# Seven half products for eight in the second channel product of two token tiles, with the cycles dealt anew

## The chip, the cores and the metric

The kernel runs on one core of a Trainium2 chip. Its time is the device time of one execution in microseconds (us). Before the change it is 352.02 us, the median of three runs (351.7 to 352.77).

## What is computed

For each of 8 batches, 12 heads, 448 positions and head size 64, sigmoid attention is followed by a token mixer and a channel mixer, without normalisation:

```python
scores = scale * np.matmul(q, k.transpose(0, 1, 3, 2)) - np.log(S)
x = np.matmul(1.0 / (1.0 + np.exp(-scores)), v)      # heads side by side: [8, 448, 768]
h = np.maximum(x.transpose(0, 2, 1) @ w_tok1, 0.0) @ w_tok2   # 448 -> 256 -> 448
u = x + h.transpose(0, 2, 1)
out = u + np.maximum(u @ w_ch1, 0.0) @ w_ch2         # 768 -> 1536 -> 768
```

The operands of TensorE are fp16, sums are fp32, and the output is fp32.

## The kernel before

A batch is cut into 3 units `u` of four heads. A **cycle** is one unit of one batch; there are 24. The order of all instructions is written out by hand: the kernel emits them in the order in which each engine is to run them, so an instruction that waits holds up everything behind it on its own engine.

In cycle (b, u), `qk` (L178) makes seven score tiles: four 64x64 matmuls each into one of two PSUM buffers of two banks (tag `qk`), and a sigmoid on ScalarE (L190) that reads the buffer out. `av` (L200) forms attention times values for the unit before in two of four other banks (`m0` to `m3`), and VectorE copies it to `xT` (L219, L223). `xtrans_dma` (L232) transposes it to `xn` by DMA from the queue of SyncE (SP). `tok_tail` and `tok1` (L257, L275) form the first token product of the unit two cycles back from `xn`; ScalarE applies the relu (L300). `ytrans` (L302) closes the cycle with the second token product, which VectorE adds to `xT` to give `ut` (L316).

After the three units, `utrans` (L321) transposes `ut` to `un` by DMA, `token_sums` (L419) forms four differences of it on VectorE, and `sevens` (L935) runs the first channel product, already as seven half products (Strassen's scheme in Winograd's form: 126 matmuls, L488), at the end of cycle u = 2. Its results leave PSUM through ScalarE (L509, L511) and VectorE (L518, L521) as `h2`.

The **second channel product** of a batch (its "lot") runs two batches later, one token tile of 128 rows per cycle. `ch2_pair` (L576) does the two column halves of tile t in cycle u = t: 64 matmuls of 64x64 in which the two halves share the array (`quads`, L356), and 16 of 128x128 (`rest`, L596). `ch2_out` (L558) adds `un` on VectorE (L561) and stores the tile. The last 64 tokens follow in cycle 2 (`ch2_last`, L611). A product of 128x128 stationary by 384 moving columns is called a **unit product** below: four 64x64 matmuls of L364 make one, one matmul of L599 or L538 is one. Tiles 0 and 1 of a lot take 2 x 2 x 12 = 48.

The loop of L1003 holds the steady cycles 9 to 23 (b = 3 to 7, lots 1 to 5), L1058 to L1092 the tail with lots 6 and 7. Lot 0 is done in cycles 5 to 8 (L875, L945), where VectorE also makes the weight sums for `sevens` (`weight_sums`, L398).

The **SP queue** issues, in one order, all `xn`, `un`, `tr_k` and `tr_q` transposes and the stores. In cycle u = 2 the order is `tr_k`, `un`, `xn`, two stores of tile 2, two of the last tokens, `tr_q`. A copy on GpSimd, the **gate** (L860), waits for `tr_q` and then lets the next loads go: v of batch b + 1, k and q of batch b + 2.

Of the kernel before, what the change touches and what calls it, by code (L numbers as in the profile page):

```python
# [21 lines left out]
NJ = 7  # L22
# [8 lines left out]
def kernel(  # L31
# [43 lines left out]
    diffs = pc.tile([128, 4, NU, NS], FP16, name="diffs")  # L75
    xTs = [pc.tile([128, NU, 2, 512], FP16, name=f"xT{n}") for n in range(2)]

    uts = [pc.tile([128, NDB, 512], FP16, name=f"ut{n}") for n in range(2)]
# [121 lines left out]
    def av(b, u, j0=0, j1=NJ):  # L200
        if j0 == 0:
            xa[b, u] = [
                bank([128, 512], FP32, f"xa_{b}_{u}_{g}")
                for g in range(2)
            ]
        ps = xa[b, u]
        for j in range(j0, j1):
            for g in range(2):
                for hi in range(2):
                    nc.tensor.matmul(  # L210
                        out=ps[g][64 * hi : 64 * hi + 64, 0:S],
                        lhsT=raw[b, "v"][64 * g : 64 * g + 64, u, hi, j, :],
                        rhs=att[b, u, j][64 * g : 64 * g + 64, hi, :],
                        start=(j == 0),
                        stop=(j == NJ - 1),
                    )
        if j1 == NJ:
            for g in range(2):
                nc.vector.tensor_copy(  # L219
                    out=xTs[b % 2][:, u, g, 0:S], in_=ps[g][:, 0:S]  # L220
                )
            if NU * b + u >= N_FIRST:
                nc.vector.tensor_copy(  # L223
                    out=xTs[b % 2][:, u, :, S:512], in_=xTs[b % 2][:, u, :, S - 64 : S]
                )


    def xn_tile(b, u):
        xn[b, u] = pa.tile([128, 2, 4, 128], FP16, tag="xn", bufs=3, name=f"xn_{b}_{u}")
        return xn[b, u]  # L230

    def xtrans_dma(b, u):  # L232
        nc.sync.dma_start_transpose(
            out=xn_tile(b, u).rearrange("s g t d -> s (g t) d"),
            in_=xTs[b % 2][:, u, :, :].rearrange("d g s -> d (g s)"),
        )

    def xtrans(b, u):
        ps = bank([128, 4, 2, 128], FP16, f"xb_{b}_{u}")
        for g in range(2):  # L240
            for t in range(4):
                nc.tensor.transpose(
                    out=ps[:, t, g, :],
                    in_=xTs[b % 2][:, u, g, 128 * t : 128 * t + 128],
                    identity=ident[:, :],
                )
# [55 lines left out]
    def ytrans(b, u, banks=()):  # L302
        for g in range(2):
            db = NU * g + u
            if banks:
                at_bank[0] = banks[g]
            ps = bank([128, 512], FP32, f"yt_{b}_{db}")
            for tcb in range(2):
                nc.tensor.matmul(  # L309
                    out=ps[:, 0:S],  # L310
                    lhsT=h1[b, u][:, tcb, g, :],
                    rhs=w2[:, tcb, :, :],
                    start=(tcb == 0),
                    stop=(tcb == 1),
                )
            nc.vector.tensor_tensor(  # L316
                out=uts[b % 2][:, db, 0:S], in0=xTs[b % 2][:, u, g, 0:S], in1=ps[:, 0:S], op=ADD
            )


    def utrans(b):  # L321
        un[b] = pa.tile([128, NDB, 4, 128], FP16, tag="un", bufs=2, name=f"un_{b}")
        nc.sync.dma_start_transpose(
            out=un[b].rearrange("s db t d -> s (db t) d"),
            in_=uts[b % 2].rearrange("d db s -> d (db s)"),
        )
# [7 lines left out]
    def ch1(b, cb, d0=0, d1=NDB):  # L334
# [5 lines left out]
        for d in range(d0, d1):  # L340
# [3 lines left out]
                rhs=uts[b % 2][:, BY_UNIT[d], 0:S],  # L344
# [27 lines left out]
    def ch1_pair(b, cb):  # L372
# [3 lines left out]
        def step(turn, n):  # L376
# [7 lines left out]
                lambda p, part: uts[b % 2][part, BY_UNIT[n], 0:S],  # L384
# [33 lines left out]

    def token_sums(b, u0=0, u1=NU):  # L419

        ut = uts[b % 2]
        k1, k2 = slice(u0, u1), slice(NU + u0, NU + u1)
        n1, n2 = slice(0, NS), slice(NS, S)
        t1, t2, t3, t4 = (diffs[:, n, u0:u1, :] for n in range(4))
# [8 lines left out]
    def ch1_seven(b, banks):  # L433
# [3 lines left out]
        ut = uts[b % 2]  # L437
# [16 lines left out]
            4: diffs[:, 3, :, :],  # L454
            5: diffs[:, 0, :, :],
            6: diffs[:, 1, :, :],
            7: diffs[:, 2, :, :],
# [72 lines left out]
    def ch2(b, t, half, n0=0, n1=NCB):  # L530
# [16 lines left out]
        if b not in un:  # L547
            for n in range(NU):
                nc.tensor.matmul(
                    out=ps[:, 128 * n : 128 * n + 128],  # L550
                    lhsT=uts[b % 2][:, NU * half + n, 128 * t : 128 * t + 128],
# [6 lines left out]
    def ch2_out(b, t, half, ps):  # L558
# [10 lines left out]
        if half == 1:  # L569
            for par in range(2):  # L570
                nc.sync.dma_start(
                    out=orow[b, 2 * t + par],
                    in_=outs[b, t][64 * par : 64 * par + 64, :],
                )

    def ch2_pair(b, t):  # L576


        outs[b, t] = pa.tile([128, D], FP32, tag="outs", bufs=3, name=f"o_{b}_{t}")
        ps = [bank([128, 512], FP32, f"c2_{b}_{t}_{p}") for p in range(2)]  # L580
        n_quads = 8

        def step(turn, n):
# [4 lines left out]
                lambda p, part, m: h2[b][  # L588
                    part, BY_GROUP[n], 128 * t + m : 128 * t + m + 64
                ],  # L590
                lambda p, part: c2[part, BY_GROUP[n], DH * p : DH * p + DH],
                n == 0,
                False,
            )

        def rest():  # L596
            for p in range(2):
                for n in range(n_quads, NCB):
                    nc.tensor.matmul(  # L599
                        out=ps[p][:, 0:DH],  # L600
                        lhsT=h2[b][:, BY_GROUP[n], 128 * t : 128 * t + 128],
                        rhs=c2[:, BY_GROUP[n], DH * p : DH * p + DH],
                        start=False,
                        stop=(n == NCB - 1),
                    )
                ch2_out(b, t, p, ps[p])

        turns = [[lambda t=t, n=n: step(t, n) for n in range(n_quads)] for t in range(2)]
        return turns[0], turns[1], rest

    def ch2_last(b, n0=0, n1=NCB):  # L611
# [20 lines left out]
        for n in range(NU if add_on_pe else 0):  # L632
            for g in range(2):
                nc.tensor.matmul(
                    out=ps[g][:, 128 * n : 128 * n + 128],
                    lhsT=uts[b % 2][:, NU * g + n, 384:448],
# [4 lines left out]
        o = pa.tile([128, DH], FP32, tag="outl", bufs=1, name=f"o_{b}_3")  # L641
# [39 lines left out]
    for n in range(2):  # L681
        nc.vector.memset(xTs[n][:, :, :, S:512], 0.0)
# [191 lines left out]
    by_half = sorted(((t, half) for t in range(3) for half in range(2)), key=lambda g: g[1])  # L874
    for c, cb in ((N_FIRST, 3), (N_FIRST + 1, 8)):  # L875
# [15 lines left out]
        for f in turn0:  # L891
            f()
        qk(b, u, 2)
# [26 lines left out]
        else:  # L920
            for w, f in pieces_ch2(0, by_half[:2]):
                f()
                if copies:
                    copies.pop(0)()
            while copies:
# [9 lines left out]
    def sevens(b, banks=(2, 3, 0, 1, 0)):  # L935
        step = ch1_seven(b, banks)
        for at, (n, gs) in enumerate(SEVENS):
            step(n, gs)
            if copies and at in (1, 3):
                copies.pop(0)()  # L940

    pending, copies = [], []
    early = weight_sums()
    lane = [0]
    for c in range(2 * NU, ONE_RUN):  # L945
# [10 lines left out]
        def work(share):  # L956
            goal = 3 * sum(shares[: c - first]) + share * shares[c - first]
            done = 0
            while pending and spent + done < total * goal / 90:
# [5 lines left out]
                done += w  # L965
                if copies:
                    copies.pop(0)()
                elif early:
                    early.pop(0)()
# [32 lines left out]

    for c in range(ONE_RUN, N_CYCLES):  # L1003
        b, u = divmod(c, NU)
        before, ahead = divmod(c - 1, NU), divmod(c - 2, NU)

        X, Y = 2, 0
        at_bank[0] = X  # L1010
        turn0, turn1, rest = ch2_pair(b - 2, u)
        part = len(turn1) * 2 // 3
        qk(b, u, 0)
        qk(b, u, 1)
        for f in turn0:
            f()
        qk(b, u, 2)
        if copies:
            copies.pop(0)()
            copies.pop(0)()  # L1020
        if u == 2:
            utrans(b - 1)
        at_bank[0] = Y
        av(*before, 0, 4)
        qk(b, u, 3)
        av(*before, 4, NJ)
        xtrans_dma(*before)
        if u == 2:
            token_sums(b - 1)
        qk(b, u, 4)  # L1030
        for f in turn1[:part]:
            f()
        qk(b, u, 5)
        for f in turn1[part:]:
            f()
        at_bank[0] = Y
        tok_tail(*ahead)
        qk(b, u, 6)
        tok1(*ahead, with_scores=True)
        rest()  # L1040
        if u == 1 and copies:
            copies.pop(0)()
            copies.pop(0)()
        if u == 0 and LATER < b + 1 < B or u == 1 and b + 1 == LATER:
            copies = through_dma(b + 1, 0)
        if u == 2:
            at_bank[0] = Y + 1
            for w, f in pieces_last(b - 2):
                f()
            sevens(b - 1)  # L1050
# [4 lines left out]
    assert not copies  # L1055


    c, lot = N_CYCLES, B - 2  # L1058
    groups = [(t, half) for t in range(3) for half in range(2)]
    work = [f for w, f in [*pieces_ch2(lot, groups), *pieces_last(lot)]]  # L1060
    before, ahead = divmod(c - 1, NU), divmod(c - 2, NU)
    at_bank[0] = X
    for f in work[:4]:
        f()
    av(*before)
    xtrans_dma(*before)
    for f in work[4:12]:
        f()
    tok1(*ahead)
    for f in work[12:20]:  # L1070
        f()
    tok1(*before)
    for f in work[20:24]:
        f()
    ytrans(*ahead)
    token_sums(B - 1, 0, 2)
    ytrans(*before)
    utrans(B - 1)
    for f in work[24:]:
        f()  # L1080
    token_sums(B - 1, 2, NU)
    at = at_bank[0]
    m = [(at + n) % 4 for n in range(4)]
    sevens(B - 1, (m[2], m[3], m[0], m[1], m[0]))
    at_bank[0] = m[1]
    for n in range(0, NCB, 3):
        ch2(B - 1, 0, 0, n, n + 3)
    for t, half in groups[1:]:
        for n in range(0, NCB, 3):
            ch2(B - 1, t, half, n, n + 3)  # L1090
# [32 lines left out]
```

## Time and profile before

| | |
|---|---|
| time, median of 3 | 352.02 us |
| profiled execution: time / span | 350.74 us / 349.0 us |
| TensorE (PE) busy | 340.3 us, 98% |
| VectorE (DVE) busy | 201.4 us, 58% |
| ScalarE (ACT) busy | 211.1 us, 60% |
| granted TensorE clock | 1.0 |
| DMA, mean over the span | 52.17 MB, 150 GB/s |

The span runs from the first to the last recorded instruction; the 1.7 us by which the time exceeds it lie around it. Engine shares are averages over an opening that waits for loads (to about 60 us), the steady cycles (102 to 298 us) and a tail. The view of the chain follows the work that ended last back to its releasers: start, length, what.

### The profile page before, as it was taken

Reading aid. Unit: us, or ns where it says so; the run is one execution under the profiler, and the core shown is the slowest. Engines: PE = TensorE matmul, PEld = TensorE weight load, DVE = VectorE, ACT = ScalarE, POOL = GpSimd, SP = SyncE. Lnnn points to the kernel's source line nnn. Section 1 sums busy time; section 2 is a strip of 40 time slices with the busy share of each in tenths; the row PEclk is TensorE's granted clock in tenths of the full one; section 3 lists DMA queues with packets and bytes.
Section 4 is the critical chain, followed back from the end, with each engine's and each line's share of the span. In section 5 each row is a group of like instructions: output and inputs, shape, how many; then the busy total and the mean of one; then the engine's idle time right before and its main releaser. Section 6 shows DMA issues by size and latency. Waiting matters only on the chain.

```text
span 349.0 us, 10254 instructions
## 1 busy us (share of the span) xinstructions
PE 340.3 (98%) x4477; PEld 239.4 (69%) x4477; DVE 201.4 (58%) x401; ACT 211.1 (60%) x271; POOL 57.3 (16%) x98
## 2 busy tenths in 40 slices
PE   7999999999999999999999999999999999999995
PEld 4655566555886679656886679656886679657963
DVE  3376467477765566458575566557574465618621
ACT  4996845587658853988348854888448854111400
POOL 8993430130040000400040000400010000000000
PEclk9999999999999999999999999999999999999999
DMA  8999999999999697998979797998985591064214
GB/s 126 165 165 192 207 204 200 169 203 246 180 183 215 93 191 148 146 185 154 196 131 188 141 190 154 147 185 148 208 124 77 88 167 24 2 121 104 55 47 113
DMA packets 104380, 52.17 MB, mean 150 GB/s; under 512 B 76432, under 2 KB 101264, under 8 KB 104336
## 3 DMA queue, kind: packets, MB, share of 16 engines
q1 hardware_dynamic: 78944, 29.70, 48.8%
q0 software_dynamic: 25168, 21.50, 40.3%
q8 instruction: 35, 0.57, 0.6%
q10 hardware_dynamic: 224, 0.33, 0.3%
q14 instruction: 9, 0.07, 0.1%
HBM read 43.45 MB, written 11.01 MB: 156 GB/s over the span
## 4 chain that ended last, share of the span: by engine, by line
PE 81%; DMA 10%; POOL 4%; ACT 2%; DVE 2%; issue 1%; ACTq 0%; POOLq 0%
PE c_ab L488 14%; PE c L364 10%; PE c L538 10%; PE c_c L488 8%; PE qk L183 7%; PE xa L210 7%; DMA xn<-xT 5%; PE c L599 5%; PE c L623 5%; PE tk L286 4%; PE yt L309 4%; DMA c<-in_moe_w_ch_dram 3%; PE c L341 3%; DMA w2s<-in_moe_w_tok_dram 2%; ACT att L190 2%; POOL raw_k L114 1%
## 5 line engine op out<-in xcount | busy, mean ns | idle before, releaser
L190 ACT ACTIVATE att<-qk,att_bias 128x896 f16<-128x896 f32 x168 | 155.4, 1017 | 35.4 <-PE qk L183 35.0
L183 PE MATMUL qk<-tr_q,tr_k 64*64 64x448 f16 x672 | 58.1, 356 | 0.5 <-ACT att L190 0.2
L219 DVE CAST xT<-xa 128x448 f16<-128x448 f32 x48 | 27.7, 619 | 41.1 <-PE xa L210 41.1
L488 PEld LDWEIGHTS <-c 128*128 128x128 f16 x504 | 47.8, 98 | 1.9 <-issue 1.8
L561 DVE TENSOR_TENSOR o<-un,c 128x384 f32<-128x384 f16 x42 | 23.3, 554 | 41.0 <-PE c L599 21.0
L364 PE MATMUL c<-c,h 64*64 64x384 f16 x960 | 46.6, 322 | 0.0
L210 PE MATMUL xa<-att,raw_v 64*64 64x448 f16 x672 | 40.7, 349 | 0.3 <-DVE ut L316 0.3
L538 PE MATMUL c<-c,h 128*128 128x384 f16 x216 | 37.8, 326 | 0.0
L509 ACT ACTIVATE pt_ab<-c_ab 128x896 f32<-128x896 f32 x21 | 19.3, 917 | 30.5 <-PE c_ab L488 30.5
L488 PEld LDWEIGHTS <-sum 128*128 128x128 f16 x378 | 36.3, 98 | 0.0
L364 PEld LDWEIGHTS <-h 64*64 64x64 f16 x960 | 28.1, 107 | 11.9
L183 PEld LDWEIGHTS <-tr_k 64*64 64x64 f16 x672 | 20.9, 105 | 19.8 <-issue 12.4
L538 PEld LDWEIGHTS <-h 128*128 128x128 f16 x216 | 20.4, 98 | 14.7 <-issue 2.1
L316 DVE TENSOR_TENSOR ut<-xT,yt 128x448 f16<-128x448 f16 x48 | 27.4, 613 | 2.9 <-PE yt L309 2.8
L210 PEld LDWEIGHTS <-raw_v 64*64 64x64 f16 x672 | 20.9, 107 | 11.6 <-issue 1.6
L860 POOL COPY gate<-tr_q 128x2 f16<-128x2 f16 x6 | 1.5, 251 | 165.1 <-DMA tr_q<-rel_q 165.1
L300 ACT ACTIVATE h<-tk 128x256 f16<-128x256 f32 x42 | 14.3, 411 | 16.7 <-PE tk L286 16.7
L599 PE MATMUL c<-c,h 128*128 128x384 f16 x120 | 22.0, 326 | 0.0
L309 PE MATMUL yt<-w,h 128*128 128x448 f16 x96 | 21.9, 353 | 0.0
L286 PE MATMUL tk<-xn,w 128*128 128x256 f16 (+1 forms) x156 | 21.8, 274 | 0.1
L511 ACT ACTIVATE h<-c_ab 128x896 f16<-128x896 f32 x7 | 6.4, 917 | 24.4 <-PE c_ab L488 24.4
L518 DVE TENSOR_TENSOR h<-pt_ab,c_ab 128x896 f16<-128x896 f32 x14 | 15.1, 1081 | 9.6 <-PE c_ab L488 9.6
(86 smaller groups left out, 418.4 us busy)
## 6 DMA issues: line engine op xcount, KB each, us to landing
out_dram<-o SPq DMA_DIRECT2D x48, 192.0 KB, 2.8
c<-in_moe_w_ch_dram POOLq DMA_DIRECT2D x4, 1152.0 KB, 15.6
raw_k<-in_k_dram POOLq DMA_DIRECT2D x10, 336.0 KB, 8.0
raw_q<-in_q_dram POOLq DMA_DIRECT2D x10, 336.0 KB, 10.4
raw_v<-in_v_dram POOLq DMA_DIRECT2D x10, 336.0 KB, 5.4
out_dram<-o SPq DMA_DIRECT2D x15, 96.0 KB, 2.6
raw_q<-in_q_dram POOLq DMA_DIRECT2D x12, 112.0 KB, 5.0
raw_k<-in_k_dram POOLq DMA_DIRECT2D x12, 112.0 KB, 4.8
```

Source lines behind the costliest of these rows:

```text
L183: nc.tensor.matmul(out=ps[64 * g : 64 * g + 64, hi, 0:S], lhsT=tr[b, "k"][64 * hi : 64 * hi + 64, u, j, 64 * g : 64 * g + 64], rhs=tr[b, " ...
L190: nc.scalar.activation(out=att[b, u, j][:, :, :], in_=ps[:, :, 0:S], func=SIGMOID, bias=bias_t[:, :], scale=att_scale,)
L210: nc.tensor.matmul(out=ps[g][64 * hi : 64 * hi + 64, 0:S], lhsT=raw[b, "v"][64 * g : 64 * g + 64, u, hi, j, :], rhs=att[b, u, j][64 * g : ...
L219: nc.vector.tensor_copy(out=xTs[b % 2][:, u, g, 0:S], in_=ps[g][:, 0:S])
L286: nc.tensor.matmul(out=ps[tcb], lhsT=w1[rows, t, cols], rhs=xn[b, u][rows, :, t, :], start=(t == 0 and not with_scores), stop=(t == (2 if ...
L309: nc.tensor.matmul(out=ps[:, 0:S], lhsT=h1[b, u][:, tcb, g, :], rhs=w2[:, tcb, :, :], start=(tcb == 0), stop=(tcb == 1),)
L316: nc.vector.tensor_tensor(out=uts[b % 2][:, db, 0:S], in0=xTs[b % 2][:, u, g, 0:S], in1=ps[:, 0:S], op=ADD)
L364: nc.tensor.matmul(out=ps[p][m : m + 64, 0:n], lhsT=lhsT(p, part, m), rhs=rhs(p, part), start=(first and turn == 0), stop=(last and turn = ...
L488: nc.tensor.matmul(out=ps[:, g, p, :], lhsT=weights[n][:, d, 128 * cb : 128 * cb + 128], rhs=moving[n][:, d, :], start=(n in (1, 5, 2) and ...
L538: nc.tensor.matmul(out=ps[:, 0:DH], lhsT=h2[b][:, BY_GROUP[cb], 128 * t : 128 * t + 128], rhs=c2[:, BY_GROUP[cb], cols], start=(cb == 0), ...
L561: nc.vector.tensor_tensor(out=outs[b, t][:, cols].rearrange("s (u d) -> s u d", d=128), in0=un[b][:, NU * half : NU * half + NU, t, :], in ...
L599: nc.tensor.matmul(out=ps[p][:, 0:DH], lhsT=h2[b][:, BY_GROUP[n], 128 * t : 128 * t + 128], rhs=c2[:, BY_GROUP[n], DH * p : DH * p + DH], ...
```

## The change

1. **Seven for eight.** From lot 1 on, tiles 0 and 1 together are a 2 x 2 block product: rows of tile 0 and 1, low and high half of the 1536 inner rows, low and high half of the 768 columns. `ch2_seven` forms it with 7 products of 6 unit products, 42 in place of 48. Products 1, 6, 7 and 4 accumulate one after the other in bank chain X, 2 in Y, 5 and 3 in Z; after each product VectorE adds the bank's running sum into the output tile (`end`, seven per lot where `ch2_out` had four). So the next product on a chain waits for that read.
2. **Sums.** Four sums of `h2` blocks per lot on VectorE (`hid`, 128x768 fp16 each), and once, in cycles 7 and 8, four sums of `c2` blocks in twelve pieces of 128x768 (`output_sums`). The weight sums start one cycle earlier.
3. **Cycles dealt anew.** The steady cycles follow `STEPS`: 6, 6 and 9 scores for 7, 7 and 7; the last tokens (`L`) move to cycle u = 1; tile 2 stays in cycle 2, now as 96 quads. `utrans` moves from behind the third score of cycle 2 to just before `sevens`, and so behind the cycle's `xn` and the stores of tile 2 on the SP queue. Tile 0 is now complete, and stored, in cycle 1.
4. **Buffers.** `xT`: one tile per unit, two in turn, for two of three units; `ut`: one buffer from batch 1 on; `un`: one for two; `xn`: two for three; `hid` shares with the differences of `token_sums`, and the last output tile with `outs`.
5. **Tail.** Lots 6 and 7 use plain 128x128 products in the orders 1 2 6 5 7 3 4 and 1 2 5 6 3 7 4.

```diff
+    class ch2_seven:
+        CHAIN = {1: "X", 6: "X", 7: "X", 4: "X", 2: "Y", 5: "Z", 3: "Z"}
...
+            self.a11, self.a12 = h[:, LOW, t0], h[:, HIGH, t0]
+            self.a21, self.a22 = h[:, LOW, t1], h[:, HIGH, t1]
+            self.weights = {1: self.a11, 2: self.a12, 4: self.a22}
+            self.moving = {
+                1: c2[:, LOW, D1], 2: c2[:, HIGH, D1], 3: c2[:, HIGH, D2],
+                5: hsums[0], 6: hsums[1], 7: hsums[2],
...
+        def sums(self, first, last):
...
+                (5, lambda: self.a21, lambda: self.a22, ADD),
+                (6, lambda: s[5], lambda: self.a11, SUB),
+                (7, lambda: self.a11, lambda: self.a21, SUB),
+                (3, lambda: self.a12, lambda: s[6], SUB),
...
+        def end(self, n):
+            b = self.b
+            t, half = {1: (0, 0), 2: (0, 0), 6: (0, 1), 3: (0, 1)}.get(n, (1, int(n != 4)))
...
+            opens = n in (1, 6, 5, 4)
+            nc.vector.tensor_tensor(
+                out=o,
+                in0=un[b][:, NU * half : NU * half + NU, t, :] if opens else o,
+                in1=self.ps[self.CHAIN[n]][:, 0:DH].rearrange("s (u d) -> s u d", d=128),
+                op=ADD,
+            )
+            if n in (3, 4):
+                store(b, t)
...
+    STEPS = (
+        "k k q6 k a4 k a7 k q6 r k t T 6 5",
+        "k k q6 k c a4 k a7 k q6 r k t T L 4 c",
+        "k k q6 k c q6 k a4 k a7 k q6 k q6 r k t k T 7",
+    )
...
+        if u == 0:
+            seven = ch2_seven(lot, X, X + 1, X + 1)
+            seven.sums(0, 2)
...
+            steps = seven.pair(((1, 2), (7, 3))[u])
...
+            elif x == "r":
+                if u == 2:
+                    outputs()
+                else:
+                    for n in ((1, 2), (3, 7))[u]:
+                        seven.end(n)
+                if u == 0:
+                    seven.sums(2, 4)
...
+            elif x == "7":
+                utrans(b - 1)
+                sevens(b - 1)
```

In `STEPS`, k is one score tile, q6 six quads steps (24 matmuls, six unit products) of the cycle's pair, a4 and a7 the parts of `av` (behind a7 come the `xT` copies and the `xn` transpose), r the ends of the pair, t and T `tok_tail` and `tok1`, c two pieces of the k and q copies for the next batch, 6, 5 and 4 plain products with their ends, L the last tokens; `ytrans` closes each cycle.

More of the change, by code (lines that the diff above doesn't have):

```diff
@@ L892 @@
             f()
+        if c > N_FIRST:
+            for n in range(3):
+                early.pop(0)()
         qk(b, u, 2)
@@ L1001 @@
     assert not copies and not pending and not early
+    X, Y = 2, 0
+    STEPS = (
[3 rows of a table added]
+    )
+    scores = ((b, u, j) for b in range(NU, B) for u in range(NU) for j in range(NJ))
     for c in range(ONE_RUN, N_CYCLES):
@@ L1005 @@
         before, ahead = divmod(c - 1, NU), divmod(c - 2, NU)
-        X, Y = 2, 0
+        lot = b - 2
+        if u == 0:
+            seven = ch2_seven(lot, X, X + 1, X + 1)
+            seven.sums(0, 2)
         at_bank[0] = X
[L1011 to L1020, printed above, removed]
-        if u == 2:
-            utrans(b - 1)
@@ L1023 @@
[L1023 to L1043, printed above, removed]
@@ L1044 @@
-        if u == 0 and LATER < b + 1 < B or u == 1 and b + 1 == LATER:
-            copies = through_dma(b + 1, 0)
[L1046 to L1050, printed above, removed]
+        if u == 2:
+            steps, outputs = ch2_pair(lot, u)
+        else:
+            steps = seven.pair(((1, 2), (7, 3))[u])
+        done = 0
+        for x in STEPS[u].split():
+            if x == "k":
+                qk(*next(scores))
+            elif x[0] == "q":
+                for n in range(int(x[1:])):
+                    steps.pop(0)()
+            elif x[0] == "a":
+                at_bank[0] = Y
+                av(*before, done, int(x[1:]))
+                done = int(x[1:])
+                if done == NJ:
+                    xtrans_dma(*before)
+                    if u == 2:
+                        token_sums(b - 1)
+            elif x == "r":
+                if u == 2:
+                    outputs()
+                else:
+                    for n in ((1, 2), (3, 7))[u]:
+                        seven.end(n)
+                if u == 0:
+                    seven.sums(2, 4)
+            elif x == "t":
+                at_bank[0] = Y
+                tok_tail(*ahead)
+            elif x == "T":
+                tok1(*ahead, with_scores=True)
+            elif x == "L":
+                at_bank[0] = X + 1
+                for w, f in pieces_last(lot):
+                    f()
+            elif x == "c":
+                for n in range(2 if copies else 0):
+                    copies.pop(0)()
+            elif x == "7":
+                utrans(b - 1)
+                sevens(b - 1)
+            else:
+                seven.plain(int(x))
@@ L1051 @@
+        assert not steps
+        if u == 0 and b + 1 < B:
+            copies = through_dma(b + 1, 0)
         at_bank[0] = Y
@@ L1054, with halves @@
             gated_loads(b)
[L1055 to L1064, printed above, removed]
+    assert not copies and not early and next(scores, None) is None
+    lot = B - 2
+    before, ahead = divmod(N_CYCLES - 1, NU), divmod(N_CYCLES - 2, NU)
+    seven = ch2_seven(lot, X, X + 1, X + 1)
+    seven.sums(0, 2)
+    def halves(b, t, half):
+        return [lambda n=n: ch2(b, t, half, n, n + 6) for n in (0, 6)]
+    seven.plain(1)
+    seven.plain(2)
+    at_bank[0] = Y
     av(*before)
     xtrans_dma(*before)
-    for f in work[4:12]:
-        f()
-    tok1(*ahead)
-    for f in work[12:20]:
-        f()
+    seven.sums(2, 4)
+    seven.plain(6)
+    seven.plain(5)
+    at_bank[0] = Y
+    tok1(*ahead)
+    for n in (7, 3, 4):
+        seven.plain(n)
+    at_bank[0] = X + 1
+    for f in halves(lot, 2, 0):
+        f()
+    at_bank[0] = Y + 1
     tok1(*before)
-    for f in work[20:24]:
-        f()
+    at_bank[0] = X
+    steps = halves(lot, 2, 1)
+    steps[0]()
+    at_bank[0] = Y
     ytrans(*ahead)
     token_sums(B - 1, 0, 2)
+    at_bank[0] = Y
     ytrans(*before)
-    utrans(B - 1)
-    for f in work[24:]:
+    steps[1]()
+    at_bank[0] = X + 1
+    for w, f in pieces_last(lot):
         f()
     token_sums(B - 1, 2, NU)
[L1082 to L1090, printed above, removed]
+    utrans(B - 1)
+    sevens(B - 1)
+    seven = ch2_seven(B - 1, Y + 1, Y, X)
+    seven.plain(1)
+    seven.sums(0, 4)
+    for n in (2, 5, 6, 3, 7, 4):
+        seven.plain(n)
+    for at, half in ((X + 1, 0), (X, 1)):
+        at_bank[0] = at
+        for f in halves(B - 1, 2, half):
+            f()
+    at_bank[0] = Y
     for w, f in pieces_last(B - 1):
```

188 lines of the change are left out of this document (139 added, 49 removed).

## Prediction

> **What bounds the kernel.** I read the engine shares first, then the chain of work that ended last, then the timelines of single engines over one batch (101 to 142 us). The page says:
>
> ```profile
> PE 340.3 (98%) x4477; PEld 239.4 (69%) x4477; DVE 201.4 (58%) x401; ACT 211.1 (60%) x271; POOL 57.3 (16%) x98
> ...
> PEclk9999999999999999999999999999999999999999
> ...
> PE 81%; DMA 10%; POOL 4%; ACT 2%; DVE 2%; issue 1%; ACTq 0%; POOLq 0%
> ```
>
> TensorE is busy in 98% of the span, at full clock, and 81% of the chain is its own. A busy row is modelled, so I look at what the chain leaves TensorE for. The chain in order of time, cycles 0 and 1 of batch 4:
>
> ```profile
> 140.76 0.76 PE yt L309 x4
> 142.02 1.30 PE c L364 x32
> 143.51 0.76 PE xa L210 x16
> 145.21 0.81 PE c L364 x20
> 146.51 8.72 DMA xn<-xT
> 155.76 0.76 PE tk L286 x6
> 156.52 1.30 PE c L599 x8
> ```
>
> The steady part is matmul behind matmul: batch 3 takes from 101.61 to 140.76, 39.15 us, with no wait. In batch 4 the chain leaves TensorE once: the `xn` of cycle 0 lands at 155.23, and the first token product of cycle 1 waits 0.46 us. Batch 6 has the same (8.78 us, from 225.27). So removed matmuls are worth their full time where nothing else comes late, and this transfer is the first thing to come late.
>
> **Step 1: the matmuls.** 32 quads take 1.30 us, so a unit product (four quads) is 0.1625 us; 8 of L599 in 1.30 us give the same, so neither form is dearer. A lot loses 48 - 42 = 6 unit products, 0.975 us. Summing the chain's pieces in the new order, from the end of `ytrans` (time F): two scores 0.50, a further score 0.19, `av` 0.76 and 0.57, t 0.11, T 0.76, L 2.07, `sevens` 12.18, `ytrans` 0.76. Cycle 0 ends at F + 8.11 (8.30 before), cycle 1 at 17.32, cycle 2 at 38.18 against 39.15. For b = 3 to 7: 5 x 0.97 = **-4.85 us**, if nothing waits.
>
> **Step 2: what could wait in the steady cycles.** ScalarE:
>
> ```profile
> 102.73 6.40 ACT L190 ACTIVATE att<-qk,att_bias 128x896 f16<-128x896 f32 x7 [0.54 <-PE qk L183]
> ```
>
> Seven sigmoids in 6.40 us: one starts every 0.90 us. In the new cycle 2 nine start from F2 + 0.36 (F2 is its start); the seventh ends at 6.8, the eighth at 7.7, the ninth at 8.6. The ninth score stands at F2 + 6.97 on TensorE, and `sevens`, which takes the eighth's buffer, at 7.92. Both just fit; the two relus (0.70 together) end at 9.2, as bank 0 is wanted again. Cost 0; it could be 0.3 a batch.
>
> VectorE:
>
> ```profile
> L561 DVE TENSOR_TENSOR o<-un,c 128x384 f32<-128x384 f16 x42 | 23.3, 554 | 41.0 <-PE c L599 21.0 <-PE c L538 18.1
> ...
> L406 DVE TENSOR_TENSOR c<-c 128x768 f16<-128x768 f16 x3 | 1.7, 553 | 0.0
> ```
>
> An end is a read of the shape of L561: 0.55 us. (Those that add an fp32 tile from SBUF have no row; below is 0.55, above the 0.62 that L518 takes for 448 such columns.) A hidden sum has the shape of L406: 0.55. A lot adds 3 ends and 4 sums, 3.9 us to a batch in which VectorE has some 16 us idle. What counts is each place. In cycle 0 the `ut` adds end at F + 1.0, sums 5 and 6 at 2.0, the `xT` copies run from 3.2 to 4.5, and end 1 is over at 5.0; product 6, which waits for it, comes at 5.40. Ends 6 and 5 are over at 7.0 and 7.9; pair (7, 3) starts at 8.61. Ends 3 and 7 are over at 13.2 and 13.7; L, which takes 3's bank, comes at 13.51, product 4 at 15.58. Each holds by 0.3 us or more: cost 0.
>
> **Step 3: the SP queue and the gate, where I see the price.** Rows before:
>
> ```profile
> 123.83 4.33 SPq L323 DMA_TRANSPOSE un<-ut  x1
> 128.27 1.25 SPq L233 DMA_TRANSPOSE xn<-xT  x1
> ...
> 132.34 3.46 SPq L138 DMA_TRANSPOSE tr_q<-rel_q  x1
> ```
> ```profile
> 139.31 0.18 POOL L860 COPY gate<-tr_q 128x2 f16<-128x2 f16 x1 [38.53 <-DMA tr_q<-rel_q]
> ```
>
> `un` went first, `tr_q` last, and the gate opened at 139.31, 2.2 us before the next F (141.52). Now `un` stands behind the stores of tile 2. Those wait for tile 2's ends, which wait behind `token_sums` (2.0 us) on VectorE: ends over at F + 26.1, stores issued until 27.3, `un` until about 31.3, and only then `tr_q`. It landed 6.8, 5.1, 6.6 and 5.0 us after its issue in the four batches: gate at 38.1 or 36.3, that is 0.1 or 1.9 us before the next F (38.18). So the first scores are still in time, `un` has landed by 34.7 (7.4 after issue) and does not hold the `ut` adds at 38.0, but the loads that the gate lets go (six of 336 KB) run some 2 us later against TensorE.
>
> The `xn` of cycle 0 travels beside these loads. It landed 15.9, 16.1 and 16.2 us after the gate in the three batches with full loads, though issued 7.2, 8.4 and 7.4 us after it: it ends with the loads. Now it is issued at F + 4.65 and wanted at F + 12.64, 8.0 us of slack where 8.3 was. Bounds: landing 16.0 after the gate, as measured, or no wait. I take 14.1, since the two stores of tile 0 (0.39 MB; the loads ran at some 200 GB/s, so 1.9 us) no longer fall into this stretch. Stall: gate + 14.1 - 12.64, 1.4 us with a late gate (b = 4, 6), none with an early one (b = 5): 2.7 us, less the 0.46 x 2 of today: **+1.8 us**.
>
> [...] The three landings, equal from the gate and not from the issue, speak rather for the end of the loads.
>
> **Step 4: the opening.** The weight sums move into idle VectorE time (51 us). In cycle 7 seven pieces of `c2` sums replace three pieces of weight sums:
>
> ```profile
> 81.04 1.15 DVE L316 TENSOR_TENSOR ut<-xT,yt 128x448 f16<-128x448 f16 x2 [0.40 <-PE yt L309]
> ```
> ```profile
> 82.24 1.51 PE L210 MATMUL xa<-att,raw_v 64*64 64x448 f16 x26 [0.15 <-DVE ut L316]
> ```
>
> `av` already waits here for the adds. The queue from 75.76 (output copies, three sums, three k copies, four sums, about 0.5 us each, and the k data that land at 78.04) now runs to 81.97: the adds and `av` come **+0.9 us** later (bounds 0 and 1.5). The last pieces fall into idle time.
>
> **Step 5: the tail.** Lot 6: minus 0.975 us, and about 0.3 back, since the four `ytrans` products now share banks 0 and 1 and the second pair waits for the adds: **-0.65**. Lot 7 has nothing between its products. After `sevens`, VectorE does end 1 (over at 1.6), then four sums (to 3.5), then ends in turn; product 5 starts at 2.2, 3 at 4.6 (end 5), 4 at 7.2 (end 7), done at 8.15, where 48 x 0.1625 = 7.8 stood: **+0.35** (bounds -0.97 and +0.9).
>
> **Sum.** -4.85 + 1.8 + 0.9 - 0.65 + 0.35 = -2.4 us. The profiled execution took 350.74 us (span 349.0 and 1.7 around it), so 348.3; it ran 1.3 under the median of 352.02, and on that the forecast is **349.6 us**.
>
> **Rivals.**
> - *A, slower: the late gate costs more than the products save.* If `xn` lands 16.0 after the gate as measured, the stalls are 3.3, 1.5 and 3.3: 8.0 - 0.9 = 7.1 on the other terms (-4.25): **+2.9, 354.9 us**. It decides from a landing of 15.1 after the gate on (5.2 of stalls gone, or 4.25 + 0.9). For it: three equal landings, and a `tr_q` more than 0.1 us later holds the scores themselves. Against it: fewer bytes in the stretch, an earlier issue. Chance 0.25.
> - *B, the full gain:* `tr_q` lands early each time, `xn` fits, and also today's 0.9 goes: -4.25 - 0.9 = -5.2, **346.9 us**. For it: two of four `tr_q` took only 5.0. Chance 0.12.
> - *C, nothing to measure:* the tight places of step 2 fail a little everywhere (0.3 for nine scores, 0.1 for buffers) on top of the stalls: 5 x 0.4 = 2.0, so -0.4, **351.6 us**. Chance 0.08.
> - That the products don't fall out is excluded: 7 x 6 x 7 = 294 unit products are written for 336.
>
> **Numbers.** Forecast 0.55, its own range 348.2 to 350.8 (stalls of 0.5 to 3). For 8 in 10 the range takes in B and C and a fifth of A: 346.9 to 352.7. A measurement of this kernel tells 0.3% (1.06 us) from no change; faster 0.67, same 0.08, slower 0.25.
>
> **What would show it.** Right: steady batches of 38.2 us without a wait; the gate's copy less than 2 us before the first scores; waits for `xn` of about 1 us at the first token product of cycle 1 in batches 4 and 6; `av` of cycle 8 about 0.9 later. Wrong: scores that wait for `tr_q` or for sigmoids in cycle 2, products 6, 3 or 4 waiting for ends in the steady cycles, or `xn` in time throughout.

## The result, and the profile after

The changed kernel takes **367.86 us** (median of 4 runs, 367.09 to 369.44) where the kernel before takes 352.19: ratio 1.045, interval 1.041 to 1.049. The forecast was 349.6 with a range to 352.7. The profiled execution took 369.44 us with a span of 367.3, 18.3 more than before. The first and fourth part of its page and the clock row answer to the lines shown of before:

```profile
PE 345.1 (94%) x4435; PEld 245.9 (67%) x4435; DVE 228.7 (62%) x462; ACT 212.6 (58%) x271; POOL 57.0 (16%) x98
...
PEclk9999999999999999969999899998999999999999
...
PE 65%; DMA 10%; DVE 2%; issue 0%
```

TensorE is busy in 94% for 98%, and it is *more* busy in us (345.1 for 340.3) with 42 instructions fewer. That can't be work; the clock row says what it is: in three slices the granted clock is below 9 tenths. (The chain is followed back only to 82.9 us here, so its shares add up to 77%. The 10% of DMA are all `xn<-xT` now; of the 10% before, `xn` was 5%.) The chain in order of time, cycles 0 and 1 of batch 3 and of batch 4 (start, length, what):

```profile
116.11 0.97 PE c L712 x24
117.39 0.76 PE tk L295 x6
118.15 2.07 PE c L753 x24
...
146.90 0.97 PE c L712 x24
148.10 12.02 DMA xn<-xT
160.60 1.40 PE tk L295 x6
161.99 3.71 PE c L753 x24
```

Here is nearly the whole loss. In batch 3 matmul follows matmul. In batch 4 the `xn` of cycle 0 takes 12.02 us, TensorE comes to stand still for it, and then the same six and 24 matmuls take 1.40 and 3.71 us where they took 0.76 and 2.07. From the start of one batch's last `ytrans` to the next, batches 3 to 7 last 39.13, 45.48, 44.21, 45.04 and 39.13 us; before they took 39.15, 39.61, 39.15, 39.68 and 39.15. So:

| | predicted | measured |
|---|---|---|
| opening, to the first score of batch 3 | +0.9 | +1.8 (104.10 for 102.30) |
| batches 3 to 7, products and deal | -4.85 | -0.02 each in b = 3 and 7 |
| batches 4 to 6 | stalls +1.8 net | **+16.3** |
| lot 6 | -0.65 | -0.32 |
| lot 7, tiles 0 and 1 | +0.35 | +0.65 |

Of the 16.3, TensorE waited 4.08, 3.40 and 4.28 us longer at the first token product than in batch 3 (11.8), and the half clock behind it took 2.28, 1.68 and 1.63 (5.6); the three waits replace 1.0 us that batches 4 and 6 lost before. The rows add up to 18.4, for 18.3 of span.

The queue of SP and the gate on GpSimd, cycle 2 of batch 3 (start, length, what; x2 are two transfers in one row, so the 11.53 us of the last row are not the length of a transfer):

```profile
130.90 1.11 SPq L589 DMA_DIRECT2D out_dram<-o  x2
132.06 4.20 SPq L332 DMA_TRANSPOSE un<-ut  x1
136.37 3.89 SPq L147 DMA_TRANSPOSE tr_q<-rel_q  x1
148.10 11.53 SPq L242 DMA_TRANSPOSE xn<-xT  x2
```
```profile
142.33 0.18 POOL L990 COPY gate<-tr_q 128x2 f16<-128x2 f16 x1 [40.19 <-DMA tr_q<-rel_q]
142.78 1.36 POOL L123 DMA_DIRECT2D raw_v<-in_v_dram  x2 [0.27 <-PE c_c L503]
144.12 1.35 POOL L123 DMA_DIRECT2D raw_k<-in_k_dram  x2
145.41 1.37 POOL L123 DMA_DIRECT2D raw_q<-in_q_dram  x2
```

`un` stands behind the stores of tile 2 and `tr_q` behind `un`; the gate opens 0.90, 1.03 and 0.31 us before the next first score, where it was 2.13, 3.37 and 2.34 before. The loads go out up to 146.8, and the `xn` follows at 148.10, 4.87 us after the first score.

### The profile page after: what moved, and what is told of

The parts are those of the page before. It is cut to its first block, busy times and chain, and to the rows that moved or that the text cites. A ratio compares the mean times of both kernels' runs of the same rounds, so it can differ in the third digit from the quotient of the medians.

```text
span 367.3 us, 10275 instructions
## 1 busy us (share of the span) xinstructions
PE 345.1 (94%) x4435; PEld 245.9 (67%) x4435; DVE 228.7 (62%) x462; ACT 212.6 (58%) x271; POOL 57.0 (16%) x98
## 4 chain that ended last, share of the span: by engine, by line
PE 65%; DMA 10%; DVE 2%; issue 0%
PE c_ab L503 13%; DMA xn<-xT 10%; PE c_c L503 8%; PE qk L192 6%; PE c L753 6%; PE c L692 6%; PE c L373 5%; PE xa L219 5%; PE c L712 4%; PE tk L295 4%; PE yt L318 3%; PE c L553 2%; PE c_a L503 1%; PE c_b L503 1%; PE tk L276 1%; DVE hid L678 0%
## 5 line engine op out<-in xcount | busy, mean ns | idle before, releaser
L192 PE MATMUL qk<-tr_q,tr_k 64*64 64x448 f16 x672 | 60.0, 359 | 0.6 <-ACT att L199 0.2
L192 PEld LDWEIGHTS <-tr_k 64*64 64x64 f16 x672 | 24.3, 105 | 23.8 <-issue 17.0
L219 PEld LDWEIGHTS <-raw_v 64*64 64x64 f16 x672 | 23.7, 107 | 9.4 <-issue 2.9
L778 DVE TENSOR_TENSOR o<-un,c 64x384 f32<-64x384 f16 x12 | 6.6, 552 | 28.2 <-PE c L753 28.0
L373 PE MATMUL c<-c,h 64*64 64x384 f16 x480 | 23.3, 322 | 0.0
L553 PE MATMUL c<-c,h 128*128 128x384 f16 x120 | 22.0, 326 | 0.0
L753 PE MATMUL c<-c,h 128*64 128x384 f16 x192 | 21.8, 387 | 0.0
L533 DVE TENSOR_TENSOR h<-pt_c,c_c 128x448 f16<-128x448 f32 x21 | 13.0, 617 | 10.6 <-PE c_c L503 10.6
L373 PEld LDWEIGHTS <-h 64*64 64x64 f16 x480 | 16.4, 107 | 3.7
```

Of the source, the lines that this page charges most:

```text
L192: nc.tensor.matmul(out=ps[64 * g : 64 * g + 64, hi, 0:S], lhsT=tr[b, "k"][64 * hi : 64 * hi + 64, u, j, 64 * g : 64 * g + 64], rhs=tr[b, " ...
L219: nc.tensor.matmul(out=ps[g][64 * hi : 64 * hi + 64, 0:S], lhsT=raw[b, "v"][64 * g : 64 * g + 64, u, hi, j, :], rhs=att[b, u, j][64 * g : ...
L373: nc.tensor.matmul(out=ps[p][m : m + 64, 0:n], lhsT=lhsT(p, part, m), rhs=rhs(p, part), start=(first and turn == 0), stop=(last and turn = ...
L533: nc.vector.tensor_tensor(out=shaped(dst), in0=shaped(parts[gs, which]), in1=ps, op=ADD)
L553: nc.tensor.matmul(out=ps[:, 0:DH], lhsT=h2[b][:, BY_GROUP[cb], 128 * t : 128 * t + 128], rhs=c2[:, BY_GROUP[cb], cols], start=(cb == 0), ...
L753: nc.tensor.matmul(out=ps[g], lhsT=h2[b][:, BY_GROUP[n], 384:448], rhs=c2[:, BY_GROUP[n], DH * g : DH * g + DH], start=(n == 0), stop=(n = ...
```

## The experiments

My theory after the result: the loads of k and q, let go 1.2 to 2.3 us later, share the DMA engines with the `xn` of cycle 0; it lands late, TensorE stands, and the standing halves its clock. Rivals: that the deal of the cycles makes TensorE wait anyway; that `xn` is slow through its buffers or the stores; that the slow matmuls have a cause of their own. In all runs the kernel before took 351.2 to 351.5 us (medians) on the same chip.

**1. The move of `utrans` alone**, in the kernel before:

```diff
-        if u == 2:
-            utrans(b - 1)
         at_bank[0] = Y
         av(*before, 0, 4)
...
+            utrans(b - 1)
             sevens(b - 1)
```


> The kernel before, with one thing changed: the un transpose stands just before sevens, behind the xn and the stores of cycle 2, as in the changed kernel. Theory 1 (late gate: un delays tr_q, the gate opens later, the loads run into the xn of cycle 0): the gate opens less than 1.5 us before the first score of the next batch (2.2 to 4.1 before), xn lands 10 to 12 us after its issue in batches 4 to 6, the first token product of cycle 1 waits 2 to 4 us in each, and the granted clock falls after the wait; 358 to 368 us. Rival theory 2 (the loss lies in the new work: more ends and sums on VectorE, nine scores in a cycle, single buffers): 352 us, within 1 us of before.

Measured: 355.56 us, ratio 1.013 (1.008 to 1.018); batches of 39.15, 40.34, 41.22, 40.16 and 39.15. The gate opened 1.36, 1.28 and 1.59 before the first score, `xn` landed 9.4, 10.3 and 9.3 us after its issue, and TensorE waited 1.2, 2.05 and 1.0 us for it, with the clock up behind each wait (T 0.76 us; mean clock 0.999). So the move alone makes the kernel slower by 4 us, nearly as much as the products were to save. The gate opened about as late as expected, but the waits were shorter and the clock stayed up: the step to 367.9 needs the rest of the change, whose gate opens another 0.3 to 1.3 us nearer to the first score.

**2. No k and q loads for batches 5 to 7** in the changed kernel (batch 4's stand in for them):

```diff
-            if b + 2 < B:
+            if b + 2 < 5:
                 load(b + 2, t, src, 0, NU)
+            elif b + 2 < B:
+                raw[b + 2, t] = raw[4, t]
```


> The changed kernel, with the k and q of batches 5, 6 and 7 not loaded (the buffers of batch 4 are read again), so that behind the gate only v moves. Theory 1: xn lands 4 to 6 us after its issue, no wait of the first token product and no fall of the clock in batches 4 to 6, each of these takes the 39.1 us of batch 3; about 350 us. Theory 2: the loss stays, above 362 us.

Measured, one execution: 351.46 us, all steady batches 39.13, `xn` 3 to 4.2 us after its issue, the clock up (T 0.76 us in every steady batch; mean clock 0.998). The chain of batch 4:

```profile
154.61 0.97 PE c L712 x24
155.88 0.76 PE tk L295 x6
156.65 2.07 PE c L753 x24
```

The loads are the cause: 16 us go with them, the half clock too, though the gate opened as late as in the changed kernel (0.99, 0.96 and 0.14 us before the first score). The same run shows the second finding. With nothing late a batch takes 39.13, and not the 38.18 of the forecast.

**3. `xn` wanted later:** the last tokens, which don't need it, ahead of t and T in cycle 1.

```diff
-        "k k q6 k c a4 k a7 k q6 r k t T L 4 c",
+        "k k q6 k c a4 k a7 k q6 r k L t T 4 c",
```


> The changed kernel, with the last tokens (L, 2.07 us) ahead of t and T in cycle 1, so that xn is wanted 2.1 us later; the same work. Theory 1: each of the three waits of 3.4 to 4.3 us shrinks by about 2.1 and the slow clock after them (1.6 to 2.3 us each) shrinks or goes; 355 to 361 us. Theory 2: within 1 us of 367.9.

Measured: 357.67 us, ratio 1.018 (1.014 to 1.023). `xn` landed 11.9, 11.4 and 12.7 us after its issue, as late as in the changed kernel; t was wanted at 15.74 after the first score and waited 1.0, 0.6 and 1.9 us, and the clock stayed up (T 0.76 us behind each; mean clock 0.999). So 2.07 us of work moved into each of three holes, 6.2 in all, are worth 10 us: the waits are shorter, and none was followed by the half clock. The move has a price: the undisturbed batches 3 and 7 take 39.71 for 39.13.

**4. `un` ahead of the stores:** the ends of tile 2 before `token_sums`, then `un`, then the stores.

```diff
...
             elif x == "r":
                 if u == 2:
+                    held.append((lot, 2))
                     outputs()
+                    utrans(b - 1)
+                    held.clear()
+                    store(lot, 2)
+                    token_sums(b - 1)
...
```


> The changed kernel, with the ends of tile 2 ahead of the token differences on VectorE and un ahead of the stores of tile 2 on the SP queue; the same work. Theory 1: un is issued 2 to 3 us earlier, the gate opens 2 to 4 us before the first score, the loads end as much earlier, and the waits shrink by 1 to 3 us each, with less of the slow clock; 352 to 362 us. Theory 2: within 1 us of 367.9.

Measured: 365.85 us, ratio 1.040 (1.035 to 1.044): mostly a miss. `un` went out 2 us earlier and `tr_q` 1.0 to 1.8, but `tr_q` then took 7.7, 6.0 and 7.5 us to land where it had taken 5.8, 5.1 and 6.3, and the gate stood at 0.32, 1.94 and 0.22 before the first score. The one batch with 1.94 is the lesson: there `xn` landed 8.9 us after its issue and TensorE waited 0.85 us; with 0.32 and 0.22 it took 12.1 and 11.8. The place of the gate decides within one execution.

**5. The deal:** two steps of `av` moved ahead of the third score, to cover a wait there.

```diff
-        "k k q6 k a4 k a7 k q6 r k t T 6 5",
+        "k k q6 a2 k a4 k a7 k q6 r k t T 6 5",
```
(and in cycles 1 and 2 the same.)


> The changed kernel, with two of seven parts of the values product (0.38 us) moved ahead of the third score in each steady cycle; the same work. If the removed products are eaten by scores that wait for the sigmoid of two scores earlier (0.1 to 0.2 us at the third score of a cycle), the undisturbed batches 3 and 7 take 0.3 to 0.5 us less than 39.13 and 38.19. Rival: they are eaten by ends and sums on VectorE that hold a bank; then these batches stay within 0.1 us. The waits for xn stay either way, so the whole is 364 to 368 us.

Measured, one execution: 366.63 us, batch 3 at 39.58 and batch 7 at 39.17 for 39.13. Neither theory held, for batch 3 got slower by 0.45: the cover moved to the third score was missing at the fifth, and cycle 2 took 21.53 us for 21.24. ScalarE shows why, cycle 0 of batch 3 of the changed kernel:

```profile
104.53 5.49 ACT L199 ACTIVATE att<-qk,att_bias 128x896 f16<-128x896 f32 x6 [0.54 <-PE qk L192]
```

Six sigmoids run back to back at 0.9 us each; a score can't start before the sigmoid two before it has ended, wherever it is put. In cycles 0 and 1 the fifth score starts 3.29 us after the first in the changed kernel and in this run alike (batch 3's first cycle apart: 3.45); in the kernel before it stands at 3.41.

**6. TensorE kept busy while it waits:** 32 useless matmuls ahead of t in cycle 1 of batches 4 to 6.

```diff
...
+        for _ in range(heated.get((b, u), 0)):
+            nc.tensor.matmul(
+                out=tks[b][0], lhsT=c1[:, 0, 0:128], ..., start=True, stop=True)
```


> The changed kernel, with 32 matmuls of 256 columns that serve nothing (some 3.5 us) just before the waiting token product of cycle 1 in batches 4, 5 and 6 (they write the bank that the product then overwrites). If the clock falls because TensorE stands still, the waits of 3.4 to 4.3 us shrink to under 1 us of standing still, xn lands as late as before (11 to 12.5 us after its issue), and the last tokens behind it run at full clock: 5 to 6 us less, 360 to 363 us. Rival: the clock falls for another reason (a budget of work), or the matmuls add to the wait; then 366 us or more.

Measured, one execution: 362.07 us, mean granted clock 1.0, batches 4 to 6 at 42.86, 42.86 and 42.93. The chain of batch 4 in that kernel:

```profile
153.97 0.97 PE c L721 x24
155.13 3.60 PE tk L275 x32
158.96 0.76 PE tk L304 x6
159.72 2.07 PE c L762 x24
```

The hole is about as long as it was, 3.7 to 3.8 us, filled with work that does nothing, and the matmuls behind it take 0.76 and 2.07 again. (In batches 4 and 6 `xn` landed 11.6 and 11.9 us after its issue, as expected; in batch 5 it took 9.7, and there the useless matmuls themselves held t.) So the half clock comes from the standing still: batches 4 to 6 take 6.1 us less, 5.6 of them the slow matmuls and 0.5 the shorter holes.

**7. q held back:** v and k go at the gate as they did; a second copy on GpSimd, which reads the landed `xn`, lets q go.

```diff
...
+                    if u == 0 and b + 1 < B:
+                        nc.gpsimd.tensor_copy(out=gate[:, :], in_=xn[before][:, 1, 3, 126:128])
+                        load(b + 1, "q", q, 0, NU)
```


> The changed kernel, with the load of q for batch b + 2 held back behind the landing of cycle 0's xn (a second gate on GpSimd that reads xn), so that only v and k run beside it; the same work. Theory 1: xn lands 5 to 9 us after its issue, in time for the 8.1 us of slack or within 1 us of it, batches 4 to 6 take 39.1 to 40 us, no fall of the clock, 350 to 354 us. Theory 2 (the loss lies in the new work): above 362 us.

Measured: 352.11 us, ratio 1.004 (1.000 to 1.007), batches of 39.13, 39.13, 39.13, 40.24 and 39.17. One load of the three, let go 11.1 to 12.7 us after the first score in batches 4 to 6, gives back 15.7 us; `xn` lands 6.0 to 7.7 us after its issue. Batch 6 shows what is late next:

```profile
223.95 9.58 DMA raw_k<-in_k_dram
234.10 0.61 DVE rel_k L134
234.71 1.07 DVE xT L228 x2
236.12 0.76 PE tk L295 x6
```

VectorE's cast of k, dealt into cycle 1, waits for its load; the `xT` copies queue behind it, and T behind those.

**8. All parts mended:** q held, the `av` steps of run 5, the sums of cycles 7 and 8 dealt into idle places, lot 7 with eight products.


> The version to which the runs point: q held back behind xn, two parts of the values product ahead of the third score, the sums of w_ch2 moved out of cycles 7 and 8 into idle VectorE time of sevens, and the last lot with eight products as in the kernel before. If the terms add (steady batches 38.7, opening 1 us less than in the changed kernel, last lot 0.65 less): 347 to 350 us, against 351.5 to 352.2 before. If the deal gives nothing: 350 to 352.

Measured: 351.83 us, ratio 1.003 (1.000 to 1.005): batches 3 to 6 of 39.43 (run 5's deal costs 0.30 each), the first score of batch 3 at 102.72, lot 7 at 11.70 us for 72 matmuls as before.

**9. A score between t and T** in cycles 0 and 1 (`r t k T` for `r k t T`), on run 8 without the `av` steps.


> The changed kernel with the q loads held behind the xn of cycle 0, the weight and output sums of the opening spread over idle places, lot 7 with eight products, and in cycles 0 and 1 a score between t and T (t k T in place of k t T). Theory: once the xn is in time, the rest of the missing 0.97 us per batch is the deal of the cycle; t followed directly by T costs 0.23 us where 0.11 was priced, so with a score between them the steady batches go from 39.13 to 38.9 us, five times 0.23 = 1.1 us; with an opening 1.6 us earlier than when q alone was held (F of batch 3 at 102.7) and 0.65 us less in lot 7, the time is 349 to 350 us, ratio 0.994 to 0.996. Rival: the score moved behind t waits for its buffer like the others, and t, now 0.2 us earlier, waits for the xn: steady batches of 39.1 to 39.4, 351 to 352 us.

Measured: 352.28 us, ratio 1.0015 (0.999 to 1.004); four batches of 39.48 and one of 39.87. A miss: worse by 0.35 a batch where I had expected 0.23 better. The score between t and T starts 4.64 us after the first where it had started at 4.45.

**10. Six useless unit products** ahead of product 5 in lots 1 to 5, on run 7.


> The changed kernel with the q loads held behind the xn of cycle 0 (352.1 us, batches of 39.13), and six useless unit products in lots 1 to 5 ahead of product 5, as many as the change takes out. Theory: the six products are worth their full 0.975 us also in this deal, and 0.95 us a batch was lost to the deal (scores waiting for sigmoids, the t switch): batches of 40.10, time 357.0. Rival: TensorE stands at the end of the cycle for something else anyway (sigmoids, VectorE), so that the matmuls taken out only made room for waiting: batches stay at 39.13 to 39.4, time 352 to 353.5.

Measured, one execution: 360.41 us, steady batches of 40.32 to 40.33, so +1.19 each: 0.97 for the six, and 0.22 that pass before product 5, in the same bank, starts behind them. (Its opening was another 2.1 us longer than run 7's; the clock was at half for 3.4 us of it, from 85.5.) So a product at this place, behind T, costs its full time and fills no hole. The run doesn't tell what one costs between the scores, where six stand ahead of the third score for eight before.

**11. The kernel before with q held** as in run 7.


> The kernel before, with the q loads of batches 4 to 7 held behind the landing of the xn of cycle 0 by a second copy on GpSimd. Theory: the q loads are what the xn shares the DMA engines with; without them it lands in 3 to 5 us, the waits of 0.46 and 0.53 us at the first token product in batches 4 and 6 go, all steady batches take 39.15, and the time falls by 1.0 us to 350.3 (ratio 0.997). Rival: q comes too late for its casts or its transposes in place of that, or the store traffic holds the xn as well: 351 to 353 us.

Measured: 351.30 us, ratio 1.001 (0.998 to 1.004); batches of 39.36, 39.15, 39.15, 39.16 and 39.15 in the profiled execution. The waits of batches 4 and 6 are gone as expected (`xn` lands 3.7 to 5.1 us after its issue); the 0.2 us more of batch 3 were not traced. The time doesn't show the gain, and the interval can't tell 1.0 us from nothing.

**12. The mended change with its own deal:** run 9 without the score moved.


> The changed kernel with its own cycles (no score or part of av moved), the q loads held behind the xn of cycle 0, the sums of the opening spread, and lot 7 with eight products. Theory: the parts add up. Steady batches of 39.13 us as when q alone was held, 0.30 less than in the run with part of av moved, five times: 351.8 - 1.5 = 350.3 us, 1.0 under the kernel before, ratio 0.997. Rival: one batch loses 1.2 us again to a late xn (batch 6 did so twice when q was held), and the time is 351 to 352, no different from the kernel before.

Measured: 350.57 us (349.96 to 352.26) against 351.33, ratio 0.9987 (0.997 to 1.0005). The batches took 39.43 (b = 3, which was not traced) and four times 39.13 in the profiled execution. It is 17 us faster than the change as made, and no different from the kernel before as far as a measurement can tell.

## Why the prediction was wrong, by its own steps

Two steps failed. Step 3's +1.8 us for the late `xn` became +16.3 and turned the sign; step 2's cost of 0 was 0.95 us a batch and took the products' gain of 0.97.

**What bounds the kernel:** right on the transfer, and stronger than I used it. "This transfer is the first thing to come late": it was. But "removed matmuls are worth their full time where nothing else comes late" fell: in batches 3 and 7, with nothing late, they were worth 0.02 us.

**Step 1 (matmuls, -4.85): the products right, the batch wrong.** Run 10 gives a unit product its price (six in 0.97 us). But the sum of the chain's pieces (38.18) left out what the pieces wait for, and that is **step 2 (cost 0)**, which failed: cycles of 8.34, 9.55 and 21.24 us where 8.11, 9.21 and 20.86 were summed, 0.95 a batch, so that 39.13 stands against 39.15. I looked for waits longer than 0.3 us at a few places and there are many of a tenth. The third score waits 0.11 us in cycles 0 and 1 and 0.18 in cycle 2 for its sigmoid, the fifth 0.10; t directly before T costs 0.23 where 0.11 was priced; in cycle 2 t and the score behind it take 0.52 for 0.30, and `sevens` starts 0.09 late. The first of these in the timeline of TensorE, cycle 0 of batch 3, before and after (quads, then the third score):

```profile
102.70 1.47 PE L364 MATMUL c<-c,h 64*64 64x384 f16 x32
104.00 0.36 PE L183 MATMUL qk<-tr_q,tr_k 64*64 64x448 f16 x4
```
```profile
104.50 1.15 PE L712 MATMUL c<-c,h 64*64 64x384 f16 x24
105.59 0.38 PE L192 MATMUL qk<-tr_q,tr_k 64*64 64x448 f16 x4
```

From start to start the 32 matmuls took 1.30 us before, their full time; the 24 now have 1.09 for the 0.97 that they need. The first sigmoid ends at 105.54, and the score follows at 105.59: the quads had been the cover of a sigmoid. What is taken out of a stretch that ScalarE paces comes back as waiting in part. The two other orders that were tried, runs 5 and 9, made no batch shorter. The ends and sums on VectorE, the other half of the step, held: no product of the steady cycles waits for one.

**Step 3 (queue and gate, +1.8): the path right, the landing mis-sized, the clock missing.** The gate fell between my two values (0.1 and 1.9). The failing term is "14.1 after the gate": it was 17.8, 17.4 and 17.5, above my upper bound of 16.0 too. That made stalls of 11.8 us where 2.7 were summed; the slower clock behind them, 5.6 us, was no term at all. I had taken 1.9 us off for two stores that leave this stretch, without a row that shows stores delaying this transfer. Runs 2 and 7 show that the loads do it. What the trace tells of the sharing, packets by queue in the 2 us from 152 and from 154 (q0 the loads, q1 the transposes):

```profile
q0 software_dynamic: 335, 0.29, 94.2%
q1 hardware_dynamic: 292, 0.07, 30.9%
```
```profile
q0 software_dynamic: 352, 0.30, 91.8%
q1 hardware_dynamic: 350, 0.09, 33.3%
```

In these 4 us the two queues move about as many packets, but a load's packet carries some 860 bytes and one of `xn` 250: `xn` gets half of the packets and a fifth of the bytes. The landing is no fixed time from the issue (3.0 to 12.3 us over the `xn` of this kernel): between 148.1 and 152 the transposes' queue moved two packets in all, the last packet of this `xn` went at 158.2, and it landed at 160.12.

Nor is it a fixed time from the gate. In both kernels and runs 1, 3, 4, 5 and 6, batches 4 to 6, it came 15.7 to 16.8 us after a gate that opened 1.3 us or more before the first score, and 16.9 to 17.8 after one that opened 1.1 or less before it. So a gate 1 us later costs over 1 us of landing. The packets show where. The last one of `xn` went 15.9, 16.8 and 15.6 us after the gate, against 15.4, 15.6 and 15.7 in the kernel before: up to there a later gate costs little more than its own delay in batches 4 and 6, and 1.2 more in batch 5. But the landing followed 1.9, 0.6 and 1.9 us behind that packet where it had followed 0.5, 0.6 and 0.4 behind it. What held it there **stays open**: in batch 4 the next cycle's `xn`, issued at 156.46, was under way by then, and so was a 16 KB packet of the instruction queue (q8, 2.3 us from 156.85). No run separates them.

Rival A had the sign, the place and two thirds of the stalls (8.0 us against 11.8); its chance of 0.25 was too low for three equal landings of 16.0. No case had the **clock**, 5.6 us, since the longest wait in the steady cycles of the trace of before was half a us. It can be read in the windows view of the changed kernel (us, busy PE, PEld, DVE, ACT, POOL, PEclk, DMA share, GB/s), batch 4 and batch 5:

```profile
156.00:158.00 2.00, 0.41 (x12) 0.01 (x3) 1.28 (x4) 1.53 (x2) 0.00 (x0) 1.00 0.80 133
158.00:160.00 2.00, 0.00 (x0) 0.00 (x0) 0.00 (x0) 0.00 (x0) 0.00 (x0) 0.61 1.32 49
160.00:162.00 2.00, 1.83 (x12) 0.95 (x14) 0.00 (x0) 0.38 (x1) 0.00 (x0) 0.50 0.77 174
162.00:164.00 2.00, 2.00 (x14) 1.15 (x16) 0.00 (x0) 0.38 (x1) 0.00 (x0) 0.50 0.26 75
164.00:166.00 2.00, 2.00 (x17) 0.99 (x14) 0.26 (x1) 0.00 (x0) 0.00 (x0) 0.68 0.00 0
```
```profile
205.50:206.00 0.50, 0.50 (x6) 0.34 (x4) 0.00 (x0) 0.13 (x1) 0.00 (x0) 1.00 1.04 184
206.00:206.50 0.50, 0.50 (x6) 0.32 (x6) 0.00 (x0) 0.50 (x2) 0.00 (x0) 0.74 0.81 307
206.50:207.00 0.50, 0.50 (x8) 0.25 (x4) 0.00 (x0) 0.08 (x1) 0.00 (x0) 0.50 0.23 86
```

In batch 4 TensorE stands from 156.4, the clock falls at 158.5 and is back at 165.3. In batch 5 it stands from 201.9 to 205.1, and the clock falls at 206.2, when it has been at work for 1.1 us.

**Step 4 (opening, +0.9): as worked out in one execution, which can't carry it.** `av` of cycle 8 came at 84.05 for 82.24. From the landing of the k data to the `ut` adds VectorE took 3.93 us for 3.00, the 0.9 of the forecast; the k data themselves came 0.9 later (78.92 for 78.04), for no reason that was traced. But over the profiled executions the first score of batch 3 starts at 102.3, 103.0 and 104.9 with the opening of before, at 102.7 to 106.7 (eight executions) with the changed one, and at 102.6 to 102.7 (three) with the sums dealt elsewhere. The two latest, 106.4 (run 10) and 106.7 (run 4), had the clock at half for 3.4 us from 85.5 and 84.7.

**Step 5 (tail): right in sign, 0.3 off in both lots.** The chain of lot 7:

```profile
348.47 0.99 PE c L692 x6
349.96 0.56 DVE hid L678
350.54 0.66 DVE hid L678 x2
352.04 0.94 DVE o L732 x2
353.02 2.12 PE c L692 x12
355.17 0.57 DVE o L732
355.78 1.14 PE c L692 x6
```

VectorE is on the chain with sums and ends, as worked out; 8.45 us stood where 8.15 were forecast and 7.8 before. Together the lots cost 0.33 where they were to save 0.30. Where lot 6 lost its 0.3 was not traced.

## What to carry to other kernels

When a DMA transfer lands with no slack beside loads that a gate releases, price a later gate by at least the landing as measured from the gate, add no relief that no row shows, and ask what is let go behind it: holding one load that isn't wanted yet was worth 15.7 us here. Where TensorE would come to stand as long as here (3.2 to 4.1 us), price the slower clock after it (1.6 to 2.3 us each) as well as the wait; useful work moved into the hole can save both (run 3). Products taken out of a stretch that another engine paces (a sigmoid every 0.9 us) are worth their time only as far as the cover they gave isn't needed.

## What the runs showed of the hardware that was not expected

In the trace of the changed kernel the clock falls at 158.5, 206.2 and 250.6 us, 47.8 and 44.4 us apart, which is 14.0 and 13.0 times 3.41 us; the stretches of half clock last 6.83, 3.41 and 3.41 us. Each fall goes with a standing of TensorE for `xn`, of 3.76, 3.20 and 4.09 us. The first fall came 2.0 us after the standing began, the others 1.1 and 0.4 us after it had ended. The waits for `xn` in runs 1 and 3, up to 2.05 us, left the clock up. What sets the times of the falls, and from how much standing on the clock falls, was not shown.
